# Queueing the first group's weight conversions three slices behind, in an attention and two gated layers on one core

## The chip, the cores and the metric

The kernel runs on one core of a Trainium2 chip. The metric is the device time of one execution in microseconds, the median of three runs. Engines are named as in the profile: PE (TensorE's matmuls), PEld (its weight loads), DVE (VectorE), ACT (ScalarE), POOL (GpSimd), and SP (the engine that issues nearly all DMAs). A "released" or "granted" clock is the clock of PE.

## The reference

For each of 4 batches and 8 heads (576 positions, 64 dimensions) causal attention is mixed with the readout of a memory; then 2304 tokens of 512 numbers run through an RMS norm and two gated layers.

```python
scores = scale * np.matmul(q, k.transpose(0, 1, 3, 2))     # causal mask, softmax, times v
mem_out = einsum(phi(q), M_prev) / (einsum(phi(q), z_prev) + 1e-6)
x = sigmoid(beta) * mem_out + (1 - sigmoid(beta)) * local  # 2304 x 512
xn = x / rms * rms_g
x = (silu(xn @ w_gate) * (xn @ w_val)) @ w_out             # first layer, d_ff 1536
x = (sigmoid(x @ w2_gate) * (x @ w2_val)) @ w2_out         # second layer, d_ff 1536
```

## The kernel before

**Groups and slices.** The tokens are worked off in five groups, `g` from -1 to 3. Group -1, the first, holds the first 128 positions of all four batches (512 columns); groups 0 to 3 hold the other 448 of one batch each. In a group each layer `l` runs over 12 slices `f` of 128 of the 1536 inner units. A slice is: 12 matmuls into `pg` and 12 into `pv` (line L803), a gated product (ACT L820, then DVE L822 and L828 in the first layer, L830 in the second), its split into a high part (ACT L835) and a residue (DVE L836), both in tile `h`, and an output share of 12 matmuls into four banks `po` (L856), which PE does after the products of the next slice. Each product is three matmuls in reduced-width float, so a weight is split too.

**Weights in group -1.** They arrive as 64-bit floats. For each slice there are three blocks, `m` = 0 (gate), 1 (value), 2 (output). A block is loaded (`raw`, `rawl`), its upper word taken by ACT (L727, `top`), joined to 32 bits by DVE (L733, `w`), stored for later (`kept`), and split into a high part by ACT (L633) and a residue by DVE (L634), into a ring of seven weight tiles (four `ws`, three `wl`). `weights(g, l, f)` does all this for the three blocks of a slice. The two first slices of group -1 are made in a stage of their own.

**Attention of the next group.** While a group runs through the layers, the attention of the next is done in steps between its slices: per head the scores `ps` (PE L206, copied by ACT L471), the exponent (L197, L199, L200), the sum with the values (`pav`), per pair of heads the memory (`pm`). The last steps make the next group's tokens: the squares (ACT L605), the inverse root (DVE L592 to L598), and for each of four tiles of tokens the norm (`att_xT`: DVE L615, ACT L619, DVE L620) and a DMA transpose (L623) into `ha`, from which the next group's first products read. Group 0's own first weights are made at that place as well (ACT L685 and L691, DVE L692; for storing `half`, DMA L696), and the outputs of group -1 leave from tile `o` (ACT L901, DVE L903, DMA L906).

**What sets the order.** A scheduler places the instructions of each engine in one fixed order, by when it thinks they are ready. The code can add an edge: what is traced in `behind(pairs)` comes, on ACT and DVE, after the given instruction of that engine. `marks` holds, for each slice since the start, the last ACT and DVE instruction traced when its gated product was made (L835 and L836). So far the edges are used in group 0 for weights, and in groups 0 and on for attention steps:

```python
def behind(pairs):
    stack = ExitStack()
    for pair in pairs:
        for i in pair:
            stack.enter_context(tc.issue_after(i))
    return stack
...
                        hidden(ws[f], l, f, n, g, xh if l == 1 and is_half(g, l, f) else xt, hs[f])
                        marks.append(tuple(last_of(e) for e in (mybir.EngineType.Activation, mybir.EngineType.DVE)))
...
                            with behind(marks[-2:-1] if g >= 0 else []):
                                steps[used]()
```

Of the kernel before, what the change touches and what calls it, by code (L numbers as in the profile page):

```python
# [56 lines left out]
def attn_moe_moe_kernel(ctx, tc, qT, kT, qk0, v, mz, beta, w8, rms_g, outT):  # L57
# [617 lines left out]
    def is_half(g, l, f):  # L675
        return g >= 0 and (l == 0 or f >= NWIDE)
# [131 lines left out]
    def hidden(w, l, f, n, g, x, h, o=0):  # L808


        pg = late["mm"].tile([128, NMAX], F32, tag="mm", name="pg")
        mm3(pg, w[0], x, n, o)
        pv = late["mm"].tile([128, NMAX], F32, tag="mm", name="pv")
        mm3(pv, w[1], x, n, o)

        t, hh = h
        t = t[:, o:o + n]
        half = is_half(g, l, f)
        u = unit[0 if l == 0 else 2][:, f]
        nc.scalar.activation(out=t, in_=pg[:, 0:n], func=AF.Tanh, scale=u[:, 0:1] if half else 0.5)  # L820
        if l == 0:
            nc.vector.scalar_tensor_tensor(out=t, in0=t, scalar=1.0, in1=pg[:, 0:n], op0=ALU.add, op1=ALU.mult)  # L822
            if half:
                nc.vector.scalar_tensor_tensor(  # L824
                    out=t, in0=t, scalar=kappa[:, f:f + 1], in1=pv[:, 0:n], op0=ALU.mult, op1=ALU.mult
                )
            else:
                nc.vector.tensor_tensor(out=t, in0=t, in1=pv[:, 0:n], op=ALU.mult)  # L828
        else:
            nc.vector.scalar_tensor_tensor(out=t, in0=t, scalar=1.0, in1=pv[:, 0:n], op0=ALU.add, op1=ALU.mult)  # L830
        if hh is None:
            return
        hi, lo = hh[:, 0, 0:n], hh[:, 1, 0:n]
        if l == 0 or g < 0:
            nc.scalar.copy(out=hi, in_=t)  # L835
            nc.vector.tensor_tensor(out=lo, in0=t, in1=hi.bitcast(F32), op=ALU.subtract)  # L836
        else:
            c = u[:, 1:2] if half else 0.5
            nc.scalar.activation(out=hi, in_=t, func=AF.Copy, scale=c)  # L839
            nc.vector.scalar_tensor_tensor(  # L840
                out=lo, in0=t, scalar=c, in1=hi.bitcast(F32), op0=ALU.mult, op1=ALU.subtract
            )

    def htiles(g, l, f):
        t = wp.tile([128, NMAX], F32, tag="t", bufs=3, name="t")
        return t, (None if plain(g, l, f) else late["h"].tile([128, 2, NMAX], F32R, tag="h", bufs=3, name="h"))

    def out_share(w, h, po, f, n):
        t, hh = h
        for d in range(KD):  # L850
            c = slice(d * 128, (d + 1) * 128)
            if hh is None:
                nc.tensor.matmul(po[d][:, 0:n], w[2][:, c], t[:, 0:n], start=(f == 0), stop=(f == NF - 1))  # L853
                continue
            for i, (a, b) in enumerate(((0, 0), (0, 1), (1, 0))):
                nc.tensor.matmul(  # L856
                    po[d][:, 0:n], w[2][:, a, c], hh[:, b, 0:n], start=(f == 0 and i == 0), stop=(f == NF - 1 and i == 2)
                )
# [54 lines left out]
    def wide_tokens(tags):  # L913

        return [xp.tile([128, KD, NMAX], F32R, tag=t, name="x" + t) for t in tags]

    def half_tokens(tag):

        t = xp.tile([128, 2, KD, NMAX], F16, tag=tag, name="h" + tag)
        return [t[:, 0], t[:, 1], t]  # L920

    def att_steps(g):
        yield lambda: att_v(g)

        for h in range(H + 1):
            if h < H:
                yield lambda h=h: att_qk(g, h)
                yield lambda h=h: att_scores(g, h)

            if h == 0:  # L930
                yield lambda: att_vmax(g)
            if h == 1:
                yield lambda: att_vsplit(g)
            if h > 0:
                yield lambda h=h: att_av(g, h - 1)
                if h % 2 == 0:
                    yield lambda h=h: att_mem(g, h // 2 - 1)
        yield lambda: att_norm(g, 0, 4)
        for t in range(4):
            yield lambda t=t: next_xT(g, t)  # L940
# [51 lines left out]
    marks = []  # L992

    def last_of(e):
        return next(i for i in reversed(nc.cur_bb.bb.instructions) if i.engine == e)
# [9 lines that stand above are left out]
    for g in range(-1, B):  # L1005
        n = 512 if g < 0 else S - 128
        steps = list(att_steps(g + 1)) if g + 1 < B else []

        total = 2 * NF - (7 if g < 0 else 6 if g == 0 else 4)

        wait = 2 if g == 0 else 1
        if g == 0:
            ring["w"] = NEARLY + NLATE
        done, used = 0, 0
        for l in range(2):
            early = 2 if g < 0 and l == 0 else 0
            ws, hs = early_ws[:early], early_hs[:early]
            for f in range(early):
                hidden(ws[f], l, f, 256, g, xt, hs[f], 256)
            po = None  # L1020
            for f in range(NF + 1):
                if f < NF:
                    if f >= early:
                        if g > 0 and l == 1 and f == NWIDE:
                            mid = NF if g < B - 1 else NF // 2 + 2
                            for e, c in ((nc.vector, slice(NWIDE, mid)), (nc.gpsimd, slice(mid, NF))):
                                if c.start < c.stop:
                                    e.tensor_scalar(
                                        out=unit[2][:, c],
                                        in0=unit[1][:, c],  # L1030
                                        scalar1=st["half_is1"],
                                        scalar2=None,
                                        op0=ALU.mult,
                                    )
                        with behind(marks[-2:-1] if g == 0 else []):
                            ws.append(weights(g, l, f))
                        hs.append(htiles(g, l, f))
                        hidden(ws[f], l, f, n, g, xh if l == 1 and is_half(g, l, f) else xt, hs[f])
                        marks.append(tuple(last_of(e) for e in (mybir.EngineType.Activation, mybir.EngineType.DVE)))
                if f > 0:  # L1040
                    if po is None:
                        po = [late[f"po{d // 2}"].tile([128, NMAX], F32, tag=f"po{d}", name="po") for d in range(KD)]
                    out_share(ws[f - 1], hs[f - 1], po, f - 1, n)
                    done += 1
                    with ExitStack() as after:

                        if g < 0 and done < 5:
                            traced = nc.cur_bb.bb.instructions
                            for e in (mybir.EngineType.Activation, mybir.EngineType.DVE, mybir.EngineType.SP):
                                after.enter_context(  # L1050
                                    tc.issue_after(next(i for i in reversed(traced) if i.engine == e))
                                )
                        while used < len(steps) and used < len(steps) * (done - wait) // (total - wait):
                            with behind(marks[-2:-1] if g >= 0 else []):
                                steps[used]()
                            used += 1
            if g < 0 and l == 0:
                begin.close()
            xn = wide_tokens("cd") if l == 0 else None
            for d in range(KD):  # L1060
                evacuate(l, d, n, g, po[d], xn)
            if l == 0 and g >= 0:
                xh = half_tokens("b")
                halve_tokens(n, po, xh)
            if l == 0 and g < 0:
                token_scale()
            xt = xn
        xt = st.pop("xt", None)
# [55 lines left out]
```

## Time and profile before

| | before |
|---|---|
| runs | 1065.26, 1063.99, 1065.15 us; median 1065.15 |
| profiled execution, device time | 1064.78 us |
| its span, from the first to the last instruction | 1063.0 us |
| mean granted clock of PE, share of full | 0.994 |
| span of group -1 in the layers, about | 60 to 283 us |

Times in the trace count from the span's start. A matmul's end is modelled, so PE counts as busy for some 0.4 us from each start, while starts of 512-column matmuls lie 0.23 us apart. "Idle before" is the time the engine stood still just ahead of an instruction, and what follows the arrow is what ended it.

### The profile page before, as it was taken

What the parts mean: (1) busy time and instruction counts of PE and PEld (TensorE: products, weight loads), DVE (VectorE), ACT (ScalarE), POOL (GpSimd) and SP (SyncE); (2) the same over time, 40 slices, a digit from 0 to 9 for tenths busy, and PEclk for the clock granted to TensorE, in tenths of its full rate; (3) what the DMA queues carried; (4) which work ended last, traced back from release to release, by engine and by line L of the source; (5) the groups of instructions that cost most, each with busy time, mean ns of one, the idle gap of its engine ahead of it and who ended that gap; (6) DMA issues with size and microseconds to landing.
All of it is one profiled execution on the core that took longest, in us unless ns stands there. A gap on an engine that the chain in (4) does not pass through costs nothing.

```text
span 1063.0 us, 17485 instructions
## 1 busy us (share of the span) xinstructions
PE 1035.8 (97%) x6477; PEld 748.4 (70%) x6477; DVE 728.6 (69%) x1556; ACT 551.3 (52%) x1042; POOL 90.1 (8%) x85
## 2 busy tenths in 40 slices
PE   8899999999899989999999999999999999999998
PEld 5768887888666767765667867657777766667665
DVE  6969999997668899873677866638788654224111
ACT  5758877675568768772454543425455432112111
POOL 3301002000001111100010110000101000000000
PEclk9999999999899999999999999999999999999999
DMA  7499998983796465769654553675455437445510
GB/s 277 156 372 371 313 367 273 323 286 124 225 317 232 139 240 188 259 230 326 205 172 160 170 184 128 160 266 185 143 177 184 142 126 213 153 142 178 170 47 35
DMA packets 89685, 222.14 MB, mean 209 GB/s; under 512 B 23808, under 2 KB 29952, under 8 KB 89472
## 3 DMA queue, kind: packets, MB, share of 16 engines
q1 hardware_dynamic: 89600, 221.03, 62.1%
q8 instruction: 51, 0.84, 0.3%
q14 instruction: 34, 0.28, 0.1%
HBM read 173.28 MB, written 44.04 MB: 204 GB/s over the span
## 4 chain that ended last, share of the span: by engine, by line
PE 85%; DVE 6%; DMA 4%; ACT 4%; issue 1%; SPq 0%; ACTq 0%; POOL 0%; DVEq 0%; POOLq 0%
PE po L856 25%; PE pg L803 25%; PE pv L803 24%; PE ps L206 4%; PE pm L576 1%; DMA out_T<-o 1%; PE pav L527 1%; PE pav L529 1%; PE pav L528 1%; DMA g_bc<-in_rms_g 1%; PE po L853 1%; DMA ha<-x 1%; DMA raw<-in_w 1%; DMA ws<-kept 0%; ACT pt L199 0%
## 5 line engine op out<-in xcount | busy, mean ns | idle before, releaser
L820 ACT ACTIVATE t<-pg,unit 128x448 f32<-128x448 f32 x88 | 55.5, 631 | 146.4 <-PE pg L803 146.4
L856 PE MATMUL po<-h,ws 128*128 128x448 f32 (+1 forms) x480 | 116.5, 384 | 3.5 <-ACT h L835 3.5
L803 PEld LDWEIGHTS <-ws 128*128 128x128 f16 x672 | 62.7, 98 | 61.5 <-issue 5.9
L803 PEld LDWEIGHTS <-wr 128*128 128x128 f16 x624 | 58.7, 99 | 61.5 <-issue 7.8
L856 PEld LDWEIGHTS po<-h,ws 128*128 128x128 f32 x480 | 89.0, 188 | 16.4 <-ACT h L835 4.5
L856 PE MATMUL po<-h,wl 128*128 128x448 f32 (+1 forms) x396 | 95.4, 384 | 0.2 <-ACT h L835 0.2
L511 POOL PARTITION_ALL_REDUCE mb<-mx x32 | 58.8, 1837 | 396.9 <-DVE mx L507 366.9
L830 DVE SCALAR_TENSOR_TENSOR t<-t,pv 128x448 f32<-128x448 f32 (+1 forms) x60 | 37.9, 632 | 78.0 <-PE pv L803 70.8
L835 ACT CAST h<-t 128x448 fp32r<-128x448 f32 (+1 forms) x70 | 40.6, 580 | 86.3 <-DVE t L824 82.0
L856 PE MATMUL po<-h,wr 128*128 128x448 f32 x372 | 85.2, 375 | 0.0
L822 DVE SCALAR_TENSOR_TENSOR t<-t,pg 128x448 f32<-128x448 f32 (+2 forms) x60 | 37.2, 620 | 69.8 <-ACT t L820 69.8
L803 PEld LDWEIGHTS <-wl 128*128 128x128 f16 x528 | 49.3, 98 | 47.0 <-issue 5.1
L856 PEld LDWEIGHTS po<-h,wl 128*128 128x128 f32 x396 | 73.8, 188 | 10.2 <-ACT h L835 0.3
L856 PEld LDWEIGHTS po<-h,wr 128*128 128x128 f32 x372 | 69.7, 188 | 6.8
L471 ACT COPY sc<-ps 128x448 f32<-128x448 f32 (+5 forms) x128 | 52.3, 421 | 38.6 <-DVE sc L466 23.4
L197 ACT ACTIVATE sc<-sc 128x1536 f32<-128x1536 f32 x32 | 47.4, 1483 | 36.3 <-DVE sc L520 36.3
L200 DVE TENSOR_TENSOR pt<-sc,pt 128x1536 f16<-128x1536 f32 x32 | 56.1, 1752 | 7.3 <-ACT pt L199 7.3
L206 PE MATMUL ps<-qq,kk 128*128 128x448 f32 (+2 forms) x160 | 57.3, 361 | 1.0 <-ACT sc L471 0.8
L836 DVE TENSOR_TENSOR h<-t,h 128x448 fp32r<-128x448 f32 (+1 forms) x70 | 46.7, 667 | 14.6 <-ACT h L835 14.2
L839 ACT ACTIVATE h<-t,unit 128x448 fp32r<-128x448 f32 x40 | 26.7, 668 | 52.3 <-DVE t L830 52.2
L824 DVE SCALAR_TENSOR_TENSOR t<-t,kappa,pv 128x448 f32<-128x448 f32 x48 | 32.6, 679 | 28.1 <-PE pv L803 27.2
L206 PE MATMUL ps<-q,kk 128*128 128x448 f32 (+2 forms) x160 | 49.4, 318 | 0.0
(260 smaller groups left out, 2443.4 us busy)
## 6 DMA issues: line engine op xcount, KB each, us to landing
raw<-in_w SPq DMA_DIRECT2D x50, 511.8 KB, 6.2
ws<-parts SPq DMA_DIRECT2D x33, 512.0 KB, 3.5
wr<-parts SPq DMA_DIRECT2D x33, 512.0 KB, 3.9
kept<-w SPq DMA_DIRECT2D x48, 256.0 KB, 5.2
wl<-parts SPq DMA_DIRECT2D x23, 512.0 KB, 3.7
rawl<-in_w SPq DMA_DIRECT2D x22, 511.8 KB, 6.7
ws<-half SPq DMA_DIRECT2D x21, 512.0 KB, 3.3
wr<-half SPq DMA_DIRECT2D x19, 512.0 KB, 3.5
```

Of the source, the lines that this page charges most:

```text
L197: nc.scalar.activation(out=sc[:, 0:n], in_=sc[:, 0:n], func=AF.Exp, scale=scale)
L200: nc.vector.tensor_tensor(out=pt[:, 1, 0:n], in0=sc[:, 0:n], in1=pt[:, 0, 0:n], op=ALU.subtract)
L206: nc.tensor.matmul(ps[:, c0:c0 + n], kk[:, k0:k0 + 128], r[:, q0:q0 + n], start=(i == 0), stop=(i == 1 and not mask))
L471: nc.scalar.copy(out=sc[:, d:d + n], in_=ps[:, c:c + n])
L511: nc.gpsimd.partition_all_reduce(mb[:, 0:448], mx[:, 0:448], channels=128, reduce_op=bass_isa.ReduceOp.max)
L803: nc.tensor.matmul(ps[:, 0:n], w[:, a, k * 128:(k + 1) * 128], x[b][:, k, o:o + n], start=(i == 0), stop=(i == 3 * KD - 1))
L820: nc.scalar.activation(out=t, in_=pg[:, 0:n], func=AF.Tanh, scale=u[:, 0:1] if half else 0.5)
L822: nc.vector.scalar_tensor_tensor(out=t, in0=t, scalar=1.0, in1=pg[:, 0:n], op0=ALU.add, op1=ALU.mult)
L830: nc.vector.scalar_tensor_tensor(out=t, in0=t, scalar=1.0, in1=pv[:, 0:n], op0=ALU.add, op1=ALU.mult)
L835: nc.scalar.copy(out=hi, in_=t)
L836: nc.vector.tensor_tensor(out=lo, in0=t, in1=hi.bitcast(F32), op=ALU.subtract)
L856: nc.tensor.matmul(po[d][:, 0:n], w[2][:, a, c], hh[:, b, 0:n], start=(f == 0 and i == 0), stop=(f == NF - 1 and i == 2))
```

## The change

In group -1, what `weights` traces for a slice is queued, on ACT and DVE, behind the cast and the residue of the hidden tile of three slices in front (`marks[-3:-2]`). The list is empty for the first slices (there are no three marks yet), so the edge begins with slice 5 of the first layer; the second layer's first slices count back into the first layer. Groups 0 to 3 keep what they had.

```diff
-                        with behind(marks[-2:-1] if g == 0 else []):
+                        with behind(marks[-2:-1] if g == 0 else marks[-3:-2] if g < 0 else []):
                             ws.append(weights(g, l, f))
```

The scheduler then orders ACT, DVE, SP and PE differently from about the third slice of group -1 to the first tiles of group 0, and the same everywhere else. Three places matter below.

**DVE at the end of group -1, before.** `t_3266` is the gated product of slice 11 of the second layer, `pv_3281` its value product, `h_3267` its hidden tile; `xn_2779`, `xn_2857`, `xn_2862`, `xn_2867` are the norms of token tiles 0 to 3.

```order
L598 SCALAR_TENSOR_TENSOR ri_2765<-nr_2768,ri_2765 128x4
L615 SCALAR_TENSOR_TENSOR xn_2779<-x_796,ri_2765,g_bc_101 128x512
L615 SCALAR_TENSOR_TENSOR xn_2857<-x_796,ri_2765,g_bc_101 128x512
L692 SCALAR_TENSOR_TENSOR wr_3336<-wr_3334,s2_3346,wr_3336 128x512 x2
L620 TENSOR_TENSOR x_796<-xn_2779,x_796 128x512
L620 TENSOR_TENSOR x_796<-xn_2857,x_796 128x512
L830 SCALAR_TENSOR_TENSOR t_3266<-t_3266,pv_3281 128x512
L615 SCALAR_TENSOR_TENSOR xn_2862<-x_796,ri_2765,g_bc_101 128x512
L615 SCALAR_TENSOR_TENSOR xn_2867<-x_796,ri_2765,g_bc_101 128x512
L836 TENSOR_TENSOR h_3267<-t_3266,h_3267 128x512
```

The same place on DVE, now:

```order
L830 SCALAR_TENSOR_TENSOR t_3266<-t_3266,pv_3281 128x512
L597 TENSOR_TENSOR nr_2768<-nr_2768,ss_2755 128x4
L598 SCALAR_TENSOR_TENSOR ri_2765<-nr_2768,ri_2765 128x4
L615 SCALAR_TENSOR_TENSOR xn_2779<-x_796,ri_2765,g_bc_101 128x512
L615 SCALAR_TENSOR_TENSOR xn_2857<-x_796,ri_2765,g_bc_101 128x512
L836 TENSOR_TENSOR h_3267<-t_3266,h_3267 128x512
L653 TENSOR_SCALAR pw_3404<-wtop_3402 128x2
L634 TENSOR_TENSOR wrl_3420<-w_3418,wrl_3420 128x512
L655 TENSOR_SCALAR inv_3406<-pw_3404 128x2
L620 TENSOR_TENSOR x_796<-xn_2779,x_796 128x512
L659 RECIPROCAL s2_3408<-inv_3406 128x2
L620 TENSOR_TENSOR x_796<-xn_2857,x_796 128x512
```

The gated product of slice 11, which stood between the norms of the two pairs of tiles, now stands ahead of all four, and of the last two steps of the root.

**DVE and SP a little later, before.** These are DVE's rows from the split of group 0's second output block on; `half` is stored from the two L692 at the end.

```order
L634 TENSOR_TENSOR wrl_3420<-w_3418,wrl_3420 128x512
L655 TENSOR_SCALAR inv_3406<-pw_3404 128x2
L620 TENSOR_TENSOR x_796<-xn_2862,x_796 128x512
L903 TENSOR_SCALAR o_3325<-po_2282 128x512
L659 RECIPROCAL s2_3408<-inv_3406 128x2
L620 TENSOR_TENSOR x_796<-xn_2867,x_796 128x512
L692 SCALAR_TENSOR_TENSOR wrl_3398<-wr_3396,s2_3408,wrl_3398 128x512 x2
```

Now DVE goes on from the second of the L620 above with these rows:

```order
L903 TENSOR_SCALAR o_3325<-po_2282 128x512
L615 SCALAR_TENSOR_TENSOR xn_2862<-x_796,ri_2765,g_bc_101 128x512
L615 SCALAR_TENSOR_TENSOR xn_2867<-x_796,ri_2765,g_bc_101 128x512
L692 SCALAR_TENSOR_TENSOR wrl_3398<-wr_3396,s2_3408,wrl_3398 128x512 x2
L620 TENSOR_TENSOR x_796<-xn_2862,x_796 128x512
L620 TENSOR_TENSOR x_796<-xn_2867,x_796 128x512
```

And these are SP's transposes and stores now:

```order
L623 DMA_TRANSPOSE ha_2778<-x_796 128x8x128 x2
L906 DMA out_T<-o_3322 512x1x128
L906 DMA out_T<-o_3325 512x1x128
L696 DMA half_0_1_3414<-wrl_3398 128x2048
L623 DMA_TRANSPOSE ha_2778<-x_796 128x8x128
L623 DMA_TRANSPOSE ha_2778<-x_796 128x8x64
```

The residues of tiles 2 and 3 (L620) and their transposes (L623) stood ahead of the two L692 and of the store of `half`, and now stand behind them.

**ACT at the change from the first layer to the second, before.** `h_1948` is the hidden tile of the first layer's last slice, `ps4_1570` the last scores of one head, `ps1_1724` the first of the next, and the rows L883 take the layer's result out of `po`.

```order
L189 ACTIVATE qq_1913<-qd_1907 128x448
L835 CAST h_1948<-t_1947 128x512
L188 ACTIVATE kk_1912<-kd_1906 128x576
L471 COPY sc_1552<-ps4_1570 128x128
L727 ACTIVATE top1_128<-rawl_2539 128x512
L727 ACTIVATE top0_126<-raw_2549 128x512
L471 COPY sc_1723<-ps1_1724 128x448
L471 COPY sc_1723<-ps2_1728 128x448
L883 ACTIVATE xc_2139<-po_722 128x512
```

Now:

```order
L189 ACTIVATE qq_1913<-qd_1907 128x448
L188 ACTIVATE kk_1912<-kd_1906 128x576
L471 COPY sc_1552<-ps4_1570 128x128
L633 ACTIVATE ws_2236<-w_2230 128x512
L633 ACTIVATE wl_2244<-w_2239 128x512
L835 CAST h_1948<-t_1947 128x512
L727 ACTIVATE top0_126<-raw_2381 128x512
L727 ACTIVATE top1_128<-raw_2391 128x512
L471 COPY sc_1723<-ps1_1724 128x448
L471 COPY sc_1723<-ps2_1728 128x448
```

L188 and the copy of `ps4_1570` moved ahead of `h_1948`; two L727, of a slice further back, still stand between it and the copy of `ps1_1724`.

## Rows read from the trace of the kernel before

**Rows 1.** The page, busy us, share of the span and instructions by engine.

```profile
PE 1035.8 (97%) x6477; PEld 748.4 (70%) x6477; DVE 728.6 (69%) x1556; ACT 551.3 (52%) x1042; POOL 90.1 (8%) x85
```

**Rows 2.** Windows of 10 and 5 us: length, busy us and count by engine, PE clock, DMA.

```profile
100.00:110.00 10.00, 10.00 (x50) 8.24 (x50) 10.00 (x19) 9.15 (x16) 0.00 (x0) 1.00 1.01 330
...
160.00:170.00 10.00, 9.03 (x68) 7.12 (x65) 9.20 (x19) 8.06 (x17) 1.60 (x1) 1.00 0.98 312
...
280.00:290.00 10.00, 5.80 (x22) 3.48 (x21) 5.12 (x11) 5.05 (x11) 0.36 (x1) 0.81 0.91 243
...
288.00:293.00 5.00, 5.00 (x15) 2.03 (x14) 0.76 (x2) 1.23 (x2) 0.00 (x0) 0.50 1.00 290
```

**Rows 3.** What PE waited for in 60:290: us in total, times, longest.

```profile
PE pg L803 <- DMA ha<-x: 4.2, 1, 4.2
PE ps L206 <- ACT sc L471: 0.8, 1, 0.8
```

**Rows 4.** Timeline of PE, end of group -1: start us, us, instruction, idle before.

```profile
277.43 0.39 PE L803 MATMUL pv<-xc,wl 128*128 128x512 f32 x1
...
280.47 2.89 PE L856 MATMUL po<-h,wl 128*128 128x512 f32 x12
287.57 4.66 PE L803 MATMUL pg<-ha,wr 128*128 128x448 f16 x12 [4.20 <-DMA ha<-x]
292.02 2.97 PE L803 MATMUL pv<-ha,wr 128*128 128x448 f16 x12
294.82 2.43 PE L803 MATMUL pg<-ha,wrl 128*128 128x448 f16 x12
```

**Rows 5.** Timeline of DVE at the same place.

```profile
273.88 0.16 DVE L598 SCALAR_TENSOR_TENSOR ri<-nr,ri 128x4 f32<-128x4 f32 x1
274.07 1.41 DVE L615 SCALAR_TENSOR_TENSOR xn<-x,ri,g_bc 128x512 f32<-128x512 f32 x2
275.40 1.41 DVE L692 SCALAR_TENSOR_TENSOR wr<-wr,s 128x512 f16<-128x512 f32 x2
276.73 1.29 DVE L620 TENSOR_TENSOR x<-xn,x 128x512 f16<-128x512 f32 x2
277.93 0.68 DVE L830 SCALAR_TENSOR_TENSOR t<-t,pv 128x512 f32<-128x512 f32 x1
278.53 1.41 DVE L615 SCALAR_TENSOR_TENSOR xn<-x,ri,g_bc 128x512 f32<-128x512 f32 x2
...
281.07 0.69 DVE L634 TENSOR_TENSOR wrl<-w,wrl 128x512 fp32r<-128x512 f32 x1
...
281.75 0.68 DVE L620 TENSOR_TENSOR x<-xn,x 128x512 f16<-128x512 f32 x1
...
283.18 0.67 DVE L620 TENSOR_TENSOR x<-xn,x 128x512 f16<-128x512 f32 x1
```

**Rows 6.** Line L623 in 270:300: ns min/median/max of issue, and us to landing.

```profile
L623 SPq DMA_TRANSPOSE ha<-x x4: 1222/1392/1742, 277.4 to 284.5; - x4
...
DMA to landing us min/median/max: 3.0/3.5/4.3
```

**Rows 7.** Timelines of DVE and PE: the last weight split and its slice's first matmul.

```profile
262.27 0.69 DVE L634 TENSOR_TENSOR wl<-w,wl 128x512 fp32r<-128x512 f32 x1
...
272.05 0.40 PE L803 MATMUL pg<-xc,wl 128*128 128x512 f32 x1
```

**Rows 8.** Timeline of ACT at the change of layers.

```profile
160.88 0.68 ACT L188 ACTIVATE kk<-kd 128x576 fp32r<-128x576 f32 x1
...
161.61 0.80 ACT L727 ACTIVATE top<-rawl 128x512 f16<-128x512 bf16 x1
```

**Rows 9.** Windows of 25 us, in group 0, columns as in rows 2.

```profile
375.00:400.00 25.00, 21.75 (x186) 16.43 (x185) 24.64 (x45) 15.86 (x28) 3.45 (x2) 1.00 0.64 231
```

**Rows 10.** Timelines of PE and DVE, a slice of the first layer.

```profile
115.49 0.39 PE L803 MATMUL pv<-xa,wl 128*128 128x512 f32 x1
...
119.44 0.67 DVE L828 TENSOR_TENSOR t<-t,pv 128x512 f32<-128x512 f32 x1
```

## The prediction

> **What bounds the kernel now.** I read the page first: it gives TensorE 1035.8 of the span's 1063.0 us [rows 1]. So the question is where PE's missing 27 us lie and whether the change touches them. The windows of 10 us show the first group's stretch: around 100 us PE, and VectorE too, are busy without a break; PE loses 0.97 us in 160:170, at the change from the first layer to the second, and 4.20 us in 280:290, where the first group ends and group 0 begins [rows 2]. The list of waits for PE over 60:290 names them: one wait of 4.2 us for the DMA that writes `ha`, and 0.8 us for a ScalarE score copy; no wait there is for a weight [rows 3]. So in this group a conversion that is ready earlier buys nothing by itself. Its cost is what it takes from the attention steps on ScalarE and VectorE, whose end is the transposed tokens `ha`.
>
> **The end of the first group, before.** PE's last product `pv` of slice 11 ends at 277.43 + 0.39 = 277.82. Two output shares follow, to 280.47 + 2.89 = 283.36, and then PE waits until 287.57 for `ha` [rows 4]. `ha` needs, for each of four token tiles, a norm on VectorE (L615), a cast on ScalarE (L619), a residue on VectorE (L620) and a DMA transpose (L623). VectorE does the first two L615 at 274.07, ahead of the gated product L830 (277.93), the other two at 278.53, and the last two L620 at 281.75 and 283.18 [rows 5]. The last one ends at about 283.85; PE starts 3.72 us after that, and 5.14 us after the third (about 282.43). The transposes take 1.2 to 1.7 us each of the SP queue, and land 3.0 to 4.3 us after issue [rows 6].
>
> **What the change does.** It adds order, no instruction and no byte. In the first group, each slice from 5 of the first layer on has its loads converted (L727, L733) and split (L633, L634) behind the cast and residue of the hidden tile of three slices before. The ring of seven weight tiles, three to a slice, already held one split in three behind the output share of that slice. So what moves is the unpacking, and the other two splits, by a part of a slice. The scheduler then places attention steps where conversions stood. Beyond the first tiles of group 0 the order is the same on every engine.
>
> *Late weights: 0.* The last slice's output block, the last of its three, is split at 262.27, and PE starts that slice's first product at 272.05 [rows 7]: about 10 us of cover, and more for the gate block. In the order after, at any slice's product at most four of VectorE's conversion steps of about 0.6 us (spacing at L830, [rows 5]) are still to be done that were done before: 2.4 us, under the cover. If the cover were gone, each late step would cost PE up to 0.6 us. DMA loads are issued later by as much; they are behind the same cover.
>
> *The layer change: -0.7 us.* Before, ScalarE casts `h`, then does L188, one score copy, two L727 (the first at 161.61), and only then the copy that frees PE's score bank [rows 8]; PE waits 0.8 us for it [rows 3]. After, L188 and the first copy come before `h`, and the two L727 stay between. L188 and that copy occupy 160.88 to 161.61 [rows 8], so the copy comes some 0.7 us sooner. The bounds are 0 (the two L727 still hold it) and -0.97, all that PE loses there [rows 2].
>
> *The end of the group: +4.4 us.* Here the order is worse. In the order after, VectorE has no L615 ahead of slice 11's L830: all four stand behind it, and L830 needs `pv`, so it can't start before 277.93, whatever has become early. From there, by the spacing of starts in rows 5: L830 0.60, two last steps of the root 0.20 each, two L615 1.33 (274.07 to 275.40), the residue of `h` 0.6: 280.9. Then the split L634, which waits for the same ScalarE work as now, 281.07 to 281.75 with a small step. Two L620 and L903 at 0.65 each and a reciprocal 0.1: 283.8. Two L615 1.33: 285.1. Two L692, which stood behind everything and now stand ahead, 1.33 (275.40 to 276.73): 286.5. Two L620: the third done at 287.15, the fourth at 287.8. ScalarE is not what is late: its second pair of casts needs the L615 at 285.1 and takes 0.6 each, done by 285.8. The fourth tile is late by 3.95 us, the third by 4.7. The SP queue has the third transpose behind the store of `half` that needs both L692, ready at 286.5, so it adds nothing more. With the delays to PE's start taken from before, PE starts at 287.8 + 3.72 = 291.5 by the fourth or 287.15 + 5.14 = 292.3 by the third. Issue alone takes each transpose 1.2 to 1.7 us, and now the last two are ready within 0.65 us of each other, so they queue behind one another on SP [rows 6]: I take 292.0, nearer the later: +4.4, bounds +3.9 and +4.7. What is late next is all of group 0, whose order is unchanged: its value loads and first products wait for the same transposes, so it shifts as a whole.
>
> *The clock: 0, up to +2.9.* PE restarts at a granted clock of 0.50, 1.2 GHz [rows 2]: its first 12 matmuls take 4.66 us and the next 12 2.97, where the 12 after them take 2.43 [rows 4]; that is 2.23 + 0.54 = 2.8 us lost. A wait of 8.6 us ends at the low clock as well. I take the same loss once more, so no change. The other bound is a loss that grows with the wait, 2.8 x 8.6 / 4.2 = 5.7, or +2.9. The Trainium skill, "TensorE: Matmul & The Clock Gate", Part 1, says the low clock is the idle state, and what PE owes on restart is a stretch of time, not a number of matmuls. By that rule the sum stays as it is, and by a loss that grows with the wait it would be 2.9 us more; no row here has a second wait of this kind to tell them apart.
>
> *Sum.* 0 - 0.7 + 4.4 + 0 = +3.7 on the profiled execution's 1064.78, so 1068.5. The median of the runs, 1065.15, lies 0.37 above that execution, so I say 1068.9. A measurement here tells about 0.2%, 2.1 us, from no change.
>
> **Rivals.**
> *Given back in group 0 (not slower).* PE idles 3.25 us in 375:400, where VectorE is busy 24.64 of 25 us [rows 9], and other waits there bring little more. If VectorE and ScalarE ran on through the longer stop instead of shifting with PE, they would be ahead by then and the wait there would vanish: 1068.9 - 3.25 = 1065.7, and with the whole layer change won 1065.4. It decides if VectorE has work to do while PE stands still. For it: that wait is VectorE's lateness. Against it: in the order its next steps behind the last tiles are products of group 0's first slice, which need PE, so it stands still too. A faster time needs PE to reach slice 11 over 2 us sooner besides, and I know of little more to win ahead of it than the 0.97 us at the layer change.
>
> *A new wait in the middle (slower still).* VectorE is full around 100 us [rows 2]. At 119.44 it starts the product of a `pv` whose last matmul ended at 115.49 + 0.39 = 115.88 [rows 10]: 3.6 us late, and PE bears some 5.8 us (an output share, 2.9 as the last in rows 4, and as many `pg` matmuls) before the next `pv` needs the bank. With the order's rows counted at the trace's durations, VectorE's work up to such a product changes by -1.5 to +1.0 us over the slices of the first layer, so it should still fit. If it doesn't, once per slice over the four fullest slices at 1 us each, the time is 1073.
>
> *The wait is hidden or doesn't grow.* This would be so if slice 11's norms were ready early and stood early; the order after has them late, so I leave it no more than the chance of a wrong reading: then only the layer change is left, 1064.4, no change that can be told.
>
> **Numbers.** Forecast 0.60, of which 0.05 ends within 0.2% (its lower bounds leave 1068.1, and a microsecond of slack in group 0 would do the rest). Given back 0.18: 0.10 same, 0.08 faster. New wait 0.12, slower. Not grown 0.10: 0.05 same, 0.05 faster, for PE also gaining in the middle. Sums: slower 0.67, same 0.20, faster 0.13. The likeliest case alone spans 1068.1 to 1072.8 (+3.9 - 0.97, and +4.7 + 2.9). The range for 8 in 10 reaches from 1064.0, into the given-back cases, to 1072.8, short of the new wait.
>
> **What would show it.** In the trace after: slice 11's L830 ahead of all four L615; the last L620 ending some 9.9 us after the last `pv` (now 6.0); PE's wait for `ha` about 8.6 us (now 4.2), with the twelve slow matmuls behind it as now; no wait for `ws` or `wl` in the first group; the 0.8 us wait on a score copy smaller; PE's idle in the 25 us that now are 375:400, shifted, still near 3 us. I am wrong if that wait is about 4 us or less, if new waits stand between 80 and 160, or if group 0 gives the time back.

## The result, and the profile after

The changed kernel is slower. Its median is 1071.09 us (five runs, 1068.06 to 1071.73); the kernel before ran beside it with a median of 1065.07. The ratio is 1.006, 95% interval 1.0039 to 1.0081. The profiled execution took 1071.09 us with a span of 1069.3, so 6.3 us more than the one of before.

The page's line of busy time by engine says where not to look. TensorE (PE) does the same work as in [rows 1] (four matmul records are missing, its weight loads are as many) and is busy 1.1 us longer; the other 5.2 us of the longer span are idle time.

```profile
PE 1036.9 (97%) x6473; PEld 749.9 (70%) x6477; DVE 727.6 (68%) x1556; ACT 550.7 (51%) x1042; POOL 89.9 (8%) x85
```

The list of waits for PE over 60:300 (us in total, times, longest) answers to [rows 3].

```profile
PE pg L803 <- DMA ha<-x: 10.3, 1, 10.3
PE ps L206 <- ACT sc L471: 1.1, 2, 0.6
PE pv L803 <- DVE t L828: 0.5, 1, 0.5
PE pg L803 <- ACT t L820: 0.2, 1, 0.2
```

One wait has grown from 4.2 to 10.3 us, and no wait for a weight has come. PE's timeline at the end of group -1 (start us, us, instruction, idle before) answers to [rows 4]:

```profile
279.13 0.39 PE L803 MATMUL pv<-xc,wl 128*128 128x512 f32 x1
279.36 2.97 PE L856 MATMUL po<-h,ws 128*128 128x512 f32 x12
282.17 2.89 PE L856 MATMUL po<-h,wl 128*128 128x512 f32 x12
295.40 4.64 PE L803 MATMUL pg<-ha,wr 128*128 128x448 f16 x12 [10.34 <-DMA ha<-x]
299.83 2.82 PE L803 MATMUL pv<-ha,wr 128*128 128x448 f16 x12
302.49 2.43 PE L803 MATMUL pg<-ha,wrl 128*128 128x448 f16 x12
```

VectorE's timeline at the same place answers to [rows 5]:

```profile
279.63 0.69 DVE L830 SCALAR_TENSOR_TENSOR t<-t,pv 128x512 f32<-128x512 f32 x1 [0.87 <-PE pv L803]
...
280.62 1.42 DVE L615 SCALAR_TENSOR_TENSOR xn<-x,ri,g_bc 128x512 f32<-128x512 f32 x2
281.95 0.68 DVE L836 TENSOR_TENSOR h<-t,h 128x512 fp32r<-128x512 f32 x1
...
285.52 1.40 DVE L615 SCALAR_TENSOR_TENSOR xn<-x,ri,g_bc 128x512 f32<-128x512 f32 x2
286.85 1.41 DVE L692 SCALAR_TENSOR_TENSOR wrl<-wr,s,wrl 128x512 f16<-128x512 f32 x2
288.17 1.28 DVE L620 TENSOR_TENSOR x<-xn,x 128x512 f16<-128x512 f32 x2
```

The gated product waits 0.87 us for PE with all four norms behind it, and the last residue (L620) ends at 289.45, 9.93 us after the last `pv` (279.13 + 0.39). From there to PE's start at 295.40 it is 5.95 us, where it was 3.72. The SP queue's timeline tells why:

```profile
284.58 3.08 SPq L623 DMA_TRANSPOSE ha<-x  x2
287.75 1.34 SPq L906 DMA_DIRECT2D out_T<-o  x2
289.18 0.61 SPq L696 DMA_DIRECT2D half<-wrl  x1
289.90 3.84 SPq L623 DMA_TRANSPOSE ha<-x  x2
```

The third tile's residue is done at about 288.8, halfway through the pair, but SP issues two output stores and the store of `half` first and reaches the third transpose at 289.90. The last two transposes then take 3.84 us to issue. This is line L623 from the third transpose on (ns min/median/max of the issue), in this kernel and in the one before:

```profile
L623 SPq DMA_TRANSPOSE ha<-x x2: 1676/1872/2068, 289.9 to 292.1; - x2
```

```profile
L623 SPq DMA_TRANSPOSE ha<-x x2: 1222/1482/1742, 282.7 to 284.5; - x2
```

Windows (length, busy us and count of PE, PEld, DVE, ACT, POOL, PE clock, DMA share, GB/s): the start, the layer change 1.5 us later than in [rows 2], the restart of PE, and the stretch of [rows 9] shifted by 7.66 us.

```profile
44.00:49.00 5.00, 4.27 (x23) 4.12 (x24) 4.59 (x10) 1.58 (x4) 2.61 (x2) 0.66 0.41 127
...
161.50:171.50 10.00, 8.87 (x53) 6.60 (x50) 8.69 (x19) 8.07 (x16) 1.60 (x1) 1.00 1.02 355
...
295.00:300.00 5.00, 4.60 (x13) 1.95 (x14) 0.00 (x0) 0.00 (x0) 0.00 (x0) 0.50 0.95 255
382.66:407.66 25.00, 21.73 (x186) 16.44 (x185) 24.64 (x45) 15.86 (x28) 3.45 (x2) 1.00 0.64 231
```

The last row is nearly that of [rows 9], to the count: group 0 runs as before, 7.66 us later. The first row is a difference that the change can't have made, since the order of instructions is the same up to about 63 us: in this execution the clock was down for part of 44 to 49 us (1.00 before), and PE begins the output shares of the second slice (the `po` of L853) at 70.24 where it was 69.25.

**Where 6.3 us came from.** 1.0 us lies ahead of anything that the change moved; 0.7 us more is lost by the last `pv` (279.13 against 277.43), 0.2 of it at the layer change and 0.5 in one wait for a `pv` bank; 6.1 us is the longer wait for `ha` (10.34 - 4.20); the slow matmuls behind it cost 0.2 us less. That makes 7.66 in group 0. About 1.3 us is won back at the ends of later groups, where PE waits 0.8 us for `ha` instead of 1.4, and 0.9 instead of 1.5 for a cast.

### The profile page after: what moved, and what is told of

Read it like the earlier page. It is cut to its first block, busy times and chain, and to the rows that moved or that the text cites. A ratio compares the mean times of both kernels' runs of the same rounds, so it can differ in the third digit from the quotient of the medians.

```text
span 1069.3 us, 17492 instructions
## 1 busy us (share of the span) xinstructions
PE 1036.9 (97%) x6473; PEld 749.9 (70%) x6477; DVE 727.6 (68%) x1556; ACT 550.7 (51%) x1042; POOL 89.9 (8%) x85
## 4 chain that ended last, share of the span: by engine, by line
PE 86%; DVE 6%; DMA 3%; ACT 3%; issue 1%; SPq 0%; POOL 0%; ACTq 0%; DVEq 0%; POOLq 0%
PE pg L803 26%; PE po L856 25%; PE pv L803 25%; PE ps L206 4%; PE pm L576 1%; PE pav L527 1%; PE pav L529 1%; PE pav L528 1%; DMA g_bc<-in_rms_g 1%; DMA out_T<-o 1%; DMA ha<-x 1%; PE po L853 1%; DMA raw<-in_w 1%; ACT h L835 0%; PE ps L210 0%
## 5 line engine op out<-in xcount | busy, mean ns | idle before, releaser
L820 ACT ACTIVATE t<-pg,unit 128x448 f32<-128x448 f32 x88 | 55.5, 631 | 152.8 <-PE pg L803 152.8
L856 PE MATMUL po<-h,ws 128*128 128x448 f32 (+1 forms) x480 | 116.1, 385 | 3.0 <-ACT h L835 3.0
L856 PEld LDWEIGHTS po<-h,ws 128*128 128x128 f32 x480 | 89.0, 188 | 15.6 <-ACT h L835 3.6
L856 PE MATMUL po<-h,wl 128*128 128x448 f32 (+1 forms) x396 | 95.3, 384 | 0.0
L856 PE MATMUL po<-h,wr 128*128 128x448 f32 x372 | 85.1, 375 | 0.0
L856 PEld LDWEIGHTS po<-h,wl 128*128 128x128 f32 x396 | 73.7, 188 | 10.2 <-ACT h L835 0.4
L856 PEld LDWEIGHTS po<-h,wr 128*128 128x128 f32 x372 | 69.7, 188 | 6.7
```

The source lines that it names most:

```text
L856: nc.tensor.matmul(po[d][:, 0:n], w[2][:, a, c], hh[:, b, 0:n], start=(f == 0 and i == 0), stop=(f == NF - 1 and i == 2))
```

## Experiments

**The theory** was that the loss is the wait for `ha`, made by the order of norms, residues and transposes at the end of group -1. **Its rivals**: the edges cost time in the middle of the group; VectorE alone sets the wait and SP adds nothing. Each run is compared with the kernel before on the same chip. Line numbers in kernels with added lines are up to four higher (L624 is L623, L860 is L856).

### The edge in one layer alone

```diff
-  ... marks[-3:-2] if g < 0 else []
+  ... marks[-3:-2] if g < 0 and l == 0 else []     # layer1
+  ... marks[-3:-2] if g < 0 and l == 1 else []     # layer2
```

> The new edge in the first layer of group -1 alone; the end of the group has the order of the kernel before on VectorE and SP. Theory (the cost is the wait for the transposed tokens at the end of the group, and its order comes from the second layer's edges): PE waits about 4.2 us for ha as before, and the time is within 0.2% of before, about 1065. Rival (the edges cost in the middle of the group, at the slices or at the layer change): PE arrives at the end 1 to 5 us later than before, 1067 to 1071, with the wait for ha still near 4.2.

> The new edge in the second layer of group -1 alone. Theory: the four norms still stand behind the gated product of slice 11, PE waits 9 to 11 us for ha, and nearly the whole loss is there: 1070 to 1073. Rival (cost in the middle, in the first layer): the wait may grow, but the time stays at 1067 or less.

Measured: layer1 1.0015 (1.0003 to 1.0026), layer2 1.0054 (1.0041 to 1.0068). PE's waits over 60:300, first layer1, then layer2:

```profile
PE pg L803 <- DMA ha<-x: 4.1, 1, 4.1
PE pg L803 <- ACT t L820: 1.9, 1, 1.9
PE ps L206 <- ACT sc L471: 1.0, 2, 0.6
```

```profile
PE pg L803 <- DMA ha<-x: 11.1, 1, 11.1
PE ps L206 <- ACT sc L471: 1.1, 1, 1.1
PE pv L803 <- DVE t L828: 0.2, 1, 0.2
```

The second layer's edges make the long wait and nearly all of the loss. The first layer's leave the wait at 4.1; they cost about a seventh of a per cent, within the 0.2% expected, and layer1's profile has a wait of 1.9 us for a ScalarE step of a gated product (L820), just after the layer change, that neither kernel has. That profiled execution took 1068.38 us and is one of the two slowest of layer1's twelve (median 1065.27), so the wait needn't stand in most of them. layer2 fell just outside its statement (a median of 1069.8 where 1070 to 1073 was expected, a wait of 11.1 where 9 to 11 was), but far from the rival's 1067 or less.

### The edge two and four slices in front

```diff
-  ... marks[-3:-2] if g < 0 else []
+  ... marks[-2:-1] if g < 0 else []     # dose2
+  ... marks[-4:-3] if g < 0 else []     # dose4
```

> The new edge two slices in front where the changed kernel has three (every slice of group -1 from the fourth on). In its order all four norms and residues of group 0's tokens stand around the gated product of slice 9 of the second layer, two slices ahead of the end, and the four transposes with them. Theory (what counts is when VectorE and SP are done with ha): no wait for ha is left, which is worth the 4.2 us of before and the slow restart of up to 2.8 us behind it, so 1057 to 1060.5, unless weights come late. Rival (weights queued only two slices in front are late): PE waits for ws, wl or a gated product in the middle of the group, in sum 4 us and more, and the time is 1064 or above.

> The new edge four slices in front. The order at the end of group -1 is nearly that of the kernel before: two norms ahead of slice 11's gated product, SP's transposes ahead of the stores; only one residue stands behind that product where it stood ahead. Theory (the order of the norms, residues and transposes at the end sets the time): wait for ha 4 to 5 us, 1064 to 1066. Rival (the edges themselves cost time in the middle): at least half of the loss stays, 1067 or more.

Measured: dose4 1.0003 (0.9991 to 1.0015), with a wait for `ha` of 4.6 us: as the theory has it, edges in every slice cost nothing that can be told while the order at the end stays. dose2 came out at 0.9997 (0.9987 to 1.0008), and neither statement held. Its waits for PE over 60:300:

```profile
PE pg L803 <- ACT xc L883: 1.7, 1, 1.7
PE pg L803 <- DVE xd L884: 1.1, 1, 1.1
PE pv L803 <- DVE t L828: 0.7, 1, 0.7
```

And the longest over 286:520, in group 0:

```profile
PE pg L803 <- ACT ws L691: 3.0, 1, 3.0
```

The wait for `ha` is gone and PE runs on at full clock from group -1 into group 0. But PE now waits at the layer change for the first layer's result (2.8 us, at a clock of 0.83 in 165:175), and group 0 waits 3.0 us for its own weights (`ws`, L691) where before waits 0.9. Most of the gain was paid back in these two places; the weights of group -1 were not late.

### Slice 11's gated product behind the first two norms

```diff
+        normed.append(last_of(mybir.EngineType.DVE))      # in att_xT, behind each L615
...
-                        hidden(ws[f], l, f, n, g, ...)
+                        with behind([normed[1:2]] if g < 0 and l == 1 and f == NF - 1 else []):
+                            hidden(ws[f], l, f, n, g, ...)
```

> The changed kernel, with the gated product of slice 11 of the second layer queued on VectorE behind the norms of token tiles 0 and 1; the SP queue gets the order of the kernel before back. Theory: the wait for ha falls from 10.3 us to between 3 and 5, and the time to about 1065 (1064 to 1066.5). Rival (VectorE is late ahead of that product as well, so the norms can't be done sooner): the gated product is late, PE waits for the hidden tile in the last output share instead, and the time stays at 1070 or more. Second rival (cost in the middle): the wait falls, the time stays over 1068.

Measured: 1.0011 (1.0002 to 1.002), median 1064.77. PE's waits over 60:300:

```profile
PE pg L805 <- DMA ha<-x: 5.1, 1, 5.1
...
PE po L858 <- DVE h L838: 0.5, 1, 0.5
```

The wait fell to 5.1, a little above the 3 to 5 expected, and the time came out in its range. With all of the change's edges in place, putting two norms back ahead takes away five sixths of the loss. This run also gives the SP queue its old order back (the transposes ahead of the stores), so it doesn't part the two; the next one does. The rival is seen in small: the root was done late, at 279.5, so the gated product started at 280.84, 1.0 us after its `pv` was ready; PE paid 0.5 us for the hidden tile, and the last residue came 7.3 us after the last `pv` instead of 6.0.

### The stores behind the transposes

```diff
+        turned.append(last_of(mybir.EngineType.SP))       # in att_xT, behind each L623
...
-        nc.sync.dma_start(out=parts[l, f], in_=pair)      # the store of half
+        with behind([turned[3:4]] if g == 0 and l == 0 and f < 2 else []):
+            nc.sync.dma_start(out=parts[l, f], in_=pair)
...
+                with behind([turned[3:4]] if g < 0 and l == 1 else []):
                     evacuate(l, d, n, g, po[d], xn)       # holds the store out_T
```

> The changed kernel, VectorE's order as it is, but on SP the stores of the outputs of group -1 and the first two stores of half queued behind the last transpose. Theory (of the wait of 10.3 us some 1.7 to 2.2 come from stores that stand ahead of the last two transposes): last residue to PE's restart 3.7 to 4.3 us where it is 5.95 now, wait for ha 8.1 to 8.8, time 1069 to 1069.8. Rival (the transposes end when the transfers in flight let them, whatever stands ahead on SP): wait still near 10.3, time 1071.

Measured: 1.0042 (1.0028 to 1.0056), median 1068.96. SP's timeline, read in two windows so that the two pairs stand apart, and then PE's:

```profile
285.95 3.07 SPq L623 DMA_TRANSPOSE ha<-x  x2
...
290.24 2.55 SPq L623 DMA_TRANSPOSE ha<-x  x2
292.84 1.34 SPq L909 DMA_DIRECT2D out_T<-o  x2
```

```profile
294.35 4.66 PE L806 MATMUL pg<-ha,wr 128*128 128x448 f16 x12 [7.93 <-DMA ha<-x]
```

VectorE's order is that of the changed kernel, and the last residue ends 9.93 us after the last `pv`, as there. It now takes 3.54 us from it to PE's start, not 5.95. So 2.4 of the 10.3 us were the SP queue's, somewhat more than the 1.7 to 2.2 expected, and the rival's 10.3 didn't come. (The times alone don't part the two: the interval overlaps that of the changed kernel.) About 1.0 of the 2.4 is the time for which the third transpose stood behind the stores: here SP issues it at 290.24, as soon as that tile is done (about 290.2), there 1.1 us after. About 1.3 is the issue of the last two transposes, 2.55 us here and 3.84 there.

### Towards a faster kernel: more norms ahead

bboth4 takes the kernel before, with the gated product behind all four norms (`normed[3:4]`) and the stores behind the transposes. aboth4 does the same to the changed kernel. bboth3 is the mildest: the kernel before, the product behind three norms (`normed[2:3]`), the stores as in bboth4. All three have the lines of the two diffs above; these differ:

```diff
-  with behind([normed[1:2]] if g < 0 and l == 1 and f == NF - 1 else []):
+  with behind([normed[3:4]] if g < 0 and l == 1 and f == NF - 1 else []):     # bboth4, aboth4
+  with behind([normed[2:3]] if g < 0 and l == 1 and f == NF - 1 else []):     # bboth3
...
-  ... marks[-3:-2] if g < 0 else []
+  ... []                                                                     # bboth4, bboth3
```

> The kernel before, without the new edge, but with slice 11's gated product queued behind all four norms, and the stores of group -1's outputs and of the first two half tiles queued behind the last transpose. The last residues stand right behind the gated product. Theory (now SP's issuing is the bound: with the transposes back to back as in the run that put the stores behind them, 8.4 us from the first issue to PE's restart, and the first can be issued at about 277.5): PE restarts near 286, wait for ha 2 to 3 us, time 1061.5 to 1063.5. Rival (only VectorE's last residue counts, some 280, and 3.6 us to the restart): wait under 0.7 us and a time of 1060 or less. Second rival: PE waits for the hidden tile, 0.5 us or more, and nothing is won.

> The changed kernel, edges of group -1 as they are, with slice 11's gated product queued behind all four norms, and the stores queued behind the last transpose. On VectorE and ScalarE group 0 has nearly the order of the kernel before (other places end in its first third). Theory (all of the loss that counts is at the end of group -1): wait for ha under 1.5 us, restart at the full clock, PE some 9 us and 2.6 us of slow matmuls sooner than in the changed kernel; with nothing given back in group 0 a time of 1058 to 1061, and with as much given back as in the run that did this to the kernel before (3.7 of 5.1 us) 1061 to 1064. Rival (the edges cost something that the wait hides): 1066 or more though the wait is gone.

> The kernel before, without the new edge, with slice 11's gated product queued behind the third norm and the stores behind the last transpose. Order differs from before in one norm, one residue and the stores only; TensorE's is the same, and so is all of group 0. The last residue ends where the last but one ended, 1.4 us sooner. Theory (last residue plus 3.7 us is PE's restart, and group 0 passes it on, since its engines stand still with PE): wait for ha 2.5 to 3.2 us and 1062.3 to 1063.3 where before has 1064. Rival (group 0 takes up what PE gains there): wait shorter as well, time within 0.05% of before.

Measured: bboth4 0.9996 (0.9986 to 1.0007), aboth4 0.9989 (0.9976 to 1.0003), bboth3 0.9986 (0.9975 to 0.9997). PE's timelines at the end of the group, of bboth4 and of aboth4:

```profile
281.08 3.26 PE L860 MATMUL po<-h,wl 128*128 128x512 f32 x12
285.17 2.43 PE L807 MATMUL pg<-ha,wr 128*128 128x448 f16 x12 [0.83 <-DMA ha<-x]
```

```profile
283.74 3.26 PE L860 MATMUL po<-h,wl 128*128 128x512 f32 x12 [2.28 <-ACT h L839]
287.82 2.43 PE L807 MATMUL pg<-ha,wr 128*128 128x448 f16 x12 [0.82 <-DMA ha<-x]
```

In both the wait is 0.8 us and PE starts at full clock. For bboth4 the theory's wait of 2 to 3 us was too long, and the first rival's (under 0.7 us) was nearly right, but not its time of 1060 or less: 3.4 us of wait and 2.8 of slow matmuls went away and the median did not move. Its waits in group 0, over 286:520, show part of where they went:

```profile
PE pav L527 <- DVE mx L507: 2.3, 1, 2.3
PE ps L206 <- ACT sc L471: 2.1, 3, 1.2
PE po L860 <- ACT o L905: 1.4, 1, 1.4
```

With the smaller ones these are 9.0 us, where the same list of before has 5.7 without `ha`. The added edges made the scheduler order group 0's attention and weight steps differently on VectorE and ScalarE, and 3.3 us more is waited there. The profiled execution shows the rest: it is 2.2 us shorter than that of before (1062.54 against 1064.78), while the medians differ by 0.2, so some 2 us of the profile's gain don't show in the runs as a whole. The theory's own error has a plain cause: its 8.4 us from the first issue to PE's restart came from turns, where 1.2 us of it is SP standing still between the pairs for the third tile. In bboth4 it is 7.3 us (277.88 to 285.17):

```profile
277.88 5.68 SPq L624 DMA_TRANSPOSE ha<-x  x4
```

aboth4 keeps more of group 0's order; there PE pays 2.3 us for slice 11's hidden tile, which stands behind four norms, and 2.5 us for two of group 0's weights (0.9 before), and it ends level with before within its interval, 0.7% under the changed kernel's ratio. That is the second case of its theory (1061 to 1064, measured 1062.31), and its rival is refuted. bboth3, whose order differs from before in one norm, one residue and the stores, is the only one whose interval lies below 1, and only just, among nine runs: by 0.14%, as large as expected, but with a wait of 3.8 us, not 2.5 to 3.2. The product stood 0.8 us behind its `pv`, and from the last residue to PE's start it took 4.09 us. The profile gives 0.4 us of shorter wait and 1.2 us of shorter restart; whether the restart is shorter in most executions was not measured, so the cause of its gain stays open.

All runs together, in us of the profiled executions:

| kernel | last `pv` to last residue | last residue to PE's start | wait for `ha` | first 12 and next 12 matmuls | ratio to before |
|---|---|---|---|---|---|
| before | 6.0 | 3.72 | 4.20 | 4.66, 2.97 | 1 |
| changed | 9.93 | 5.95 | 10.34 | 4.64, 2.82 | 1.006 |
| layer1 | 6.03 | 3.61 | 4.09 | 4.10, 2.43 | 1.0015 |
| layer2 | 12.04 | 4.63 | 11.13 | 3.96, 2.43 | 1.0054 |
| dose2 | ended 10.3 ahead of it | (none) | none | 2.44, (split) | 0.9997 |
| dose4 | 5.61 | 4.52 | 4.59 | 4.66, 2.95 | 1.0003 |
| norms | 7.34 | 4.06 | 5.08 | 4.02, 2.43 | 1.0011 |
| turns | 9.93 | 3.54 | 7.93 | 4.66, 2.85 | 1.0042 |
| bboth4 | 3.31 | 3.60 | 0.83 | 2.43, 2.43 | 0.9996 |
| aboth4 | 5.59 | 3.58 | 0.82 | 2.43, 2.43 | 0.9989 |
| bboth3 | 5.28 | 4.09 | 3.79 | 3.98, 2.43 | 0.9986 |

## Why the prediction was right, and what was mis-sized

The direction and its mechanism were right: the order at the end of group -1 makes the tokens late, and group 0 shifts as a whole. Undoing that order with all edges in place (norms) takes five sixths of the loss away; the second layer's edges alone (layer2), which make such an order, bring nine tenths of it. The size was +3.7 where +6.0 was measured, inside the range. By its steps:

- *Late weights, 0.* Right: no wait for `ws` or `wl` in group -1.
- *The layer change, -0.7.* Wrong. PE loses 1.13 us in the ten microseconds there, before 0.97 [rows 2]. The prediction counted L188 and one copy as moved ahead of `h`, but the order it read also put two L633 there, some 1.06 us of ScalarE. The two L727 start at 162.28 (before 161.61 [rows 8]), and with PE 1.0 us later in this execution the copy came only 0.3 us sooner; then a second copy was waited for. Two waits, 0.49 and 0.62, stand for one of 0.8.
- *The end of the group, +4.4, bounds +3.9 to +4.7.* This is the mis-sized term: the wait grew by 6.14. The VectorE part was exact, 9.9 us forecast from last `pv` to last residue and 9.93 measured, and its rows came where the sum has them. VectorE's share of the growth is 3.9 us, as forecast; from the last residue to PE's start it is 2.2 (5.95 - 3.72), where the forecast had about 0.5. The step that failed is "The SP queue has the third transpose behind the store of `half` that needs both L692, ready at 286.5, so it adds nothing more". The two output stores stand there too. SP was at them from 287.75 to 289.09 and at `half` until 289.79, 1.0 us after the third residue; and the two transposes behind them took 2.07 and 1.68 us to issue, where in the kernel before they took 1.74 and 1.22. The run turns measures this share: 2.4 us of wait.
- *The clock, 0, up to +2.9.* Right, with some luck: 4.64 + 2.82 us for the first 24 matmuls against 4.66 + 2.97. Four of the other runs lose 1.1 us less there (last section), and these two executions happened to be alike. The runs now hold what the prediction lacked, other waits of this kind. Between waits of 3.8 and 11.1 us the loss is 1.5 to 2.8 us and doesn't grow with the wait; the longest has one of the smallest. The Trainium skill, "TensorE: Matmul & The Clock Gate", Part 1, has it that a restart owes a stretch of time, not a number of matmuls. The traces agree in so far as the loss doesn't follow the wait.
- *Given back in group 0.* Refuted for this change: 3.27 us of idle PE stand there (before 3.25), 7.66 us later; VectorE and ScalarE do nothing either in 295:300, where PE restarts. In the other direction the runs showed it: of what bboth4 won at the end of group -1, group 0 took about half back, where its order differed.
- *A new wait in the middle.* Only 0.5 us, once, for a `pv` bank. What the first layer's edges cost by themselves is 0.15% in layer1, where the order differs from the changed kernel's; in dose4 it is nothing that can be told.

The forecast and the result also differ by 1.0 us of the profiled execution that lies ahead of anything the change moved, and by 1.3 us that later groups gave back, which no step had.

## What to carry to other kernels

An edge that only holds back work with slack still re-deals every queue after it: read the new order at the next place where all engines meet, and count there from the last event that nothing can move. Count the DMA queue like an engine, each store ahead of the critical transfer with its issue time, and two transfers that become ready together one after the other. And a removed wait is worth what the next bound leaves of it: here some 6 us won at one boundary (dose2, bboth4, aboth4) came to 0 to 1.2 us in the medians, none of it clear of the noise.

## What the hardware showed that was not expected

- The restart of PE after waiting for `ha` cost either about 1.6 us (first 12 matmuls 3.96 to 4.10 us, the next at 2.43) or about 2.7 (4.64 to 4.66, then 2.82 to 2.97), with waits of 3.8 to 11.1 us in the first kind and 4.2 to 10.3 in the second. After 0.8 us it cost nothing. From PE's start the granted clock is 0.50 (1.2 GHz) for 3.1 to 3.4 us in the first kind and for about 5.2 to 5.5 in the second, for instance over 293.2:296.5 in layer1 and 287.57:293 in before, and 1.00 (2.4 GHz) after it. What decides between the two was not tried.
- The clock also fell beside shorter waits: it is 0.83 in 172:182 of layer1, behind a wait of 1.9 us, and in 165:175 of dose2, with waits of 1.7 and 1.1. But it stayed at 1.00 over 300:500 of before, with a wait of 2.0 us in it.
- One transpose takes SP 1.22 to 2.07 us to issue. Of the eleven that SP issued straight behind a load or a store (over the eleven traces), nine took 1.64 to 2.07; of the others all but two took 1.22 to 1.45. But layer2 has one right behind two output stores that took 1.31. Why some are slower was not tried.
- The granted clock fell at 44 to 49 us in the changed kernel's profiled execution and not in that of before (0.66 against 1.00), with the same order of instructions up to there. It was down at that place in dose4's as well (0.83 over 40:50) and not in layer1's (1.00): about 1 us in the changed kernel's execution that the change didn't make.
